# Second MLP layer in five matmuls for six, whole phase tables and wider VectorE operations, in a fused S4D and channel-MLP kernel

## The chip, the cores and the metric

One core of one Trainium2 chip runs the whole program. Its engines are TensorE (PE in the profile), VectorE (DVE), ScalarE (ACT), GpSimd (POOL) and SyncE (SP, which here only issues DMAs); each takes its own instructions in order, and semaphores tie them together. The metric is device microseconds from the start of the program to its end; the median of several runs counts. Float32 results are needed, so the MLP's matmuls run on operands that were split into a rounded high part and a low part (type fp32r).

## The reference

```python
x = A_u                                     # (1, 2048, 576)
xn = layernorm(x)
s = S4D(xn)      # K = 2 Re(sum_n C exp(A dt l)), causal convolution by FFT over 2048 tokens, + xn * D_skip
y = layernorm(xn)
h = gelu(y @ w1 + b1)                       # 576 -> 4608
g = silu(h @ w2 + b2)                       # 4608 -> 576
return x + s * g
```

The MLP reads layer-normed tokens, S4D convolves each of the 576 channels with its own kernel, and the two meet only in the last line.

## The kernel before

**Slots.** The MLP is cut into 48 slots. A slot takes a group of 512 tokens (TB) and 384 hidden units (G = 3 tiles of 128). Its first layer (`layer1`, L599) is three runs of 14 matmuls of 512 columns, each followed by gelu (L635) and by the split into `hh` (ACT, L638) and `hl` (DVE, L641). Its second layer (`layer2`, L662) makes four token tiles j of 128 tokens; for each of the three hidden tiles and each half of the 576 output columns it issues `hh*w2h`, `hh*w2l` and `hl*w2h`, three matmuls of 288 columns: 72 in a slot. Results go to PSUM tiles `mxa` and `mxb` (two banks each, taken in turn), and DVE adds each finished one to `acc` (L672, 576 columns). A bank can be written again only when that add has read it.

**S4D work.** Between the MLP's matmuls stand the parts of S4D: for each block of 16 channels a table (`tables`: phases, sine and cosine on ACT, products on DVE, in tiles `w`, `v`, `U`, `mg`), from which PE makes the convolution kernel (`kgen`, L978); for each of six chunks of 96 channels the transform of x (`x1`, L1082), of the kernel (`k1`, L1113), a second stage and product (`s2`, L1143; `copy`, `prod`, `sums`), the inverse (L1185) and the last transform (`i1`, L1211). `i1`'s two halves are copied out by ACT (L1219) and stored to `s_s` in DRAM by POOL's queue (L1220).

**The end.** For tokens 0 to 7 of each group of 16 (tiles b 0 to 7) the gate is finished half-way through the kernel and `combine` (loads L701 to L703, two DVE operations L709 and L710, stores L713) makes their output. Tiles 8 to 15 wait for the last two slots: `last_s` loads one tile of s from DRAM (SP's queue, L724, 288 KB, each into its place in `A`), and `finish` makes the gate from `acc` (ACT L745, DVE L750 to L756), multiplies, adds x (L760) and issues two stores of 64 rows (L763). The last tile, 15, is done in two halves of 288 columns, straight from PSUM.

**Order.** The program traces itself through a planner (`Order`): each piece is a `step` with an engine, a cost in us, needs and marks; `advance` takes steps in the order of the time that the plan gives them, urgent ones (due times `by`) ahead. The order of each engine's instructions, and of each DMA queue's issues, is fixed by that plan when the program is built. `pe_turns` decides where PE takes a piece of S4D: `pace` and `END` spread the chunks, `DUE` and `ALONE` say when a `kgen` may stand by itself; where it can, it rides ahead of another piece (`ride`). `LEN` holds the planned length of the parts of a slot's second layer, `add_by` when an add must be done. `pair` (L582) does two half-height matmuls of a coming slot at once.

**Memory.** `tile_pool` names share memory: equal names take turns in `bufs` buffers. A table needs its `w` from one of two buffers, and the single `v` and `U`, which are free only when the `kgen` of the block before has run. `row` has four buffers, for `combine` and `finish` alike.

Of the kernel before, what the change touches and what calls it, by code (L numbers as in the profile page):

```python
# [18 lines left out]
P = 128  # L19
# [16 lines left out]
TB = 512  # L36

def dve(n):  # L40
    return 0.075 + 0.00104 * n
# [169 lines left out]
def mixer_kernel(ctx, tc, u, log_a_real, a_imag, c_real, c_imag, log_dt, d_skip, w1, b1, w2, b2,  # L211
# [38 lines left out]
    idp = sb.tile([P, P], F32, name="idp")  # L250
# [112 lines left out]

    def table_memory():

        t = [sb.tile([P, 2, SB, NV], F32, name="w", bufs=2) for _ in range(2)]
        t = [x.rearrange("p k c t -> p (k c t)") for x in t + [sb.tile([P, 2, SB, 64], F32, name="v")]]
        return [t[k // 3][:, k % 3 * D:(k % 3 + 1) * D] for k in range(8)]
# [163 lines left out]
    def split_raw(low_on=nc.vector):  # L532
# [4 lines left out]
        if which == 1:  # L537
            if i == 0 and k:
                w1_tiles()
            h, lo, r1, r2 = W[1]  # L540
            h, lo = (h[:, i], lo[:, i]) if i < KB else (r1, r2)
        else:
            if i == 0:
                W[2] = (sb.tile([P, G, D], F32R, name="w2h"), sb.tile([P, G, D], F32R, name="w2l"))
            h, lo = W[2]
            h, lo = h[:, i], lo[:, i]
# [97 lines left out]
    def layer2(g, tb, j, terms, last, alone=False):  # L644
# [3 lines left out]
        h, lo = W[2]  # L648
# [7 lines left out]
        if alone:  # L656
            z = q[:, terms[0][1], :288]
            nc.tensor.matmul(z, IDM[0], acc[:, tb * 4 + j, terms[0][1] * 288:][:, :288], start=True, stop=False)
        for i, dh in terms:
            d = slice(dh * 288, dh * 288 + 288)  # L660
            for k, (a, b) in enumerate(((hh, h), (hh, lo), (hl, h))):
                nc.tensor.matmul(q[:, dh, :288], a[:, i, c], b[:, i, d], start=i == 0 and k == 0 and not alone,  # L662
                                 stop=i == G - 1 and k == 2)
        if last:
            Q2.pop(j)
        if alone:
            return z

        def add(dh, n):
            o = acc[:, tb * 4 + j].rearrange("p (h d) -> p h d", h=2)[:, dh:dh + n]  # L670
            b = BIAS[0].rearrange("p (h d) -> p h d", h=2)[:, dh:dh + n] if g == 0 else o
            nc.vector.tensor_add(o, q[:, dh:dh + n, :288], b)  # L672
# [97 lines left out]
    def params():  # L770
# [8 lines left out]
        dt = sb.tile([P, 2, SB, 32], F32, name="U").rearrange("p a b c -> p (a b c)")[:, :D]  # L779
# [108 lines left out]
    def tables(b):  # L888
# [5 lines left out]
        def phase(k):  # L894
            if k == 0:
                T["w"] = sb.tile([P, 2, SB, NV], F32, name="w", bufs=2)
# [28 lines left out]
        def weigh(k, part):  # L925

            if k == 0 and part == 0:
                T["v"] = sb.tile([P, 2, SB, 64], F32, name="v")
                T["U"] = sb.tile([P, 2, SB, 32], F32, name="U")
                TAB[b] = (T["U"], T["v"])  # L930
            w, v, m = T["w"], T["v"], T["m"]
            if part == 0:
                nc.vector.tensor_mul(T["U"][:, k], w[:, k, :, 33:], m[:, :, 64:])
            elif part == 1:
                nc.vector.tensor_mul(v[:, k, :, :32], w[:, k, :, 32:0:-1], m[:, :, :32])
            elif k == 0:
                nc.vector.tensor_mul(v[:, k, :, 32:], w[:, k, :, :32], m[:, :, 32:64])
            else:
                nc.vector.scalar_tensor_tensor(v[:, k, :, 32:], w[:, k, :, :32], -1.0, m[:, :, 32:64],
# [6 lines left out]
                 step("DVE", dve(SB * NV), f(phase, 0), need=[("wu", b - 2, 1)] if b > 1 else []),  # L946
# [6 lines left out]
                + [step("DVE", dve(n), f(weigh, k, part), need=[("sin", b, k)] + ([("kg", b - 1)] if b else []),  # L953
                        mark=("wu", b, k) if part == 2 else None) for k in range(2) for part in range(3)])
# [10 lines left out]
    def kgen(b):  # L965
# [20 lines left out]
        return [step("PE", KG + 0.2, mm, need=need + [("wu", b, 1)], cv=1, mark=("kg", b)),  # L986
# [23 lines left out]
    def chunk(c):  # L1010
# [41 lines left out]
        def in_parts(which, i, get, m, need):  # L1052

            def high():
# [655 lines left out]
```

## Time and profile before

| | us |
|---|---|
| median of 3 runs (1099.77 to 1100.17) | 1099.98 |
| span of the profiled execution | 1099.5 |
| PE busy / DVE busy / ACT busy / POOL busy in it | 1090.1 / 920.5 / 696.6 / 184.6 |
| start of the last slot's second layer on PE, in it | 1082.63 |
| start of the last `i1` on PE, in it | 1024.69 |

The profile covers one execution, first to last instruction; its own time is that span, half a microsecond under the median of the timed runs. Matmuls are pipelined and the end of each is modelled, so the pace of PE is read from the distance of starts, and not from the duration of one. DVE's records also overlap: a following operation starts some 0.08 us before the record of the one before ends. The chain of waits follows the work that ended last back through what released it.

### The profile page before, as it was taken

Reading aid. Unit: us, or ns where it says so; the run is one execution under the profiler, and the core shown is the slowest. Engines: PE = TensorE matmul, PEld = TensorE weight load, DVE = VectorE, ACT = ScalarE, POOL = GpSimd, SP = SyncE. Lnnn points to the kernel's source line nnn. Section 1 sums busy time; section 2 is a strip of 40 time slices with the busy share of each in tenths; the row PEclk is TensorE's granted clock in tenths of the full one; section 3 lists DMA queues with packets and bytes.
Section 4 is the critical chain, followed back from the end, with each engine's and each line's share of the span. In section 5 each row is a group of like instructions: output and inputs, shape, how many; then the busy total and the mean of one; then the engine's idle time right before and its main releaser. Section 6 shows DMA issues by size and latency. Waiting matters only on the chain.

```text
span 1099.5 us, 27206 instructions
## 1 busy us (share of the span) xinstructions
PE 1090.1 (99%) x11447; PEld 953.9 (87%) x11447; DVE 920.5 (84%) x1514; ACT 696.6 (63%) x1040; POOL 184.6 (17%) x254
## 2 busy tenths in 40 slices
PE   9999999999999999999999999999999999999997
PEld 7989899889888888888998888888888888888896
DVE  7798678979998899999999998898998986765356
ACT  6585699866666675676865857566675754325233
POOL 5566211170110100001100000000100012110220
PEclk9999999999999999999999999999999999999999
DMA  8746655734444152455623314242333426453453
GB/s 230 235 144 156 232 162 196 215 75 126 154 124 145 48 112 57 116 121 143 150 57 94 91 56 126 39 147 60 90 92 77 143 65 180 117 177 108 126 149 94
DMA packets 139683, 138.23 MB, mean 126 GB/s; under 512 B 88952, under 2 KB 105016, under 8 KB 138984
## 3 DMA queue, kind: packets, MB, share of 16 engines
q1 hardware_dynamic: 124664, 85.49, 29.5%
q0 software_dynamic: 14336, 50.12, 14.8%
q8 instruction: 89, 1.46, 0.6%
q10 hardware_dynamic: 560, 0.89, 0.3%
q14 instruction: 34, 0.28, 0.1%
HBM read 102.17 MB, written 36.63 MB: 126 GB/s over the span
## 4 chain that ended last, share of the span: by engine, by line
PE 96%; SPq 1%; DMA 1%; DVE 1%; issue 0%; ACT 0%; ACTq 0%; DVEq 0%
PE mxb L662 21%; PE mxa L662 21%; PE mxa L599 20%; PE mxb L599 20%; PE cv L1143 3%; PE cv L978 3%; PE cv L1185 2%; PE cv L1211 2%; PE cv L1113 1%; PE cv L1082 1%; DMA w<-in_A_u_dram 1%; SPq L791 1%; PE mxa L614 0%; SPq L383 0%; DMA acc<-in_A_u_dram 0%
## 5 line engine op out<-in xcount | busy, mean ns | idle before, releaser
L641 DVE TENSOR_TENSOR hl<-h,hh 128x512 fp32r<-128x512 f32 x144 | 99.1, 691 | 88.3 <-ACT hh L638 87.6
L662 PE MATMUL mxb<-w2h,hh 128*128 128x288 f32 x576 | 171.6, 298 | 0.0
L662 PE MATMUL mxa<-w2h,hh 128*128 128x288 f32 x573 | 170.8, 298 | 0.0
L662 PE MATMUL mxb<-w2h,hl 128*128 128x288 f32 x576 | 170.1, 295 | 0.3 <-DVE hl L641 0.3
L662 PE MATMUL mxb<-w2l,hh 128*128 128x288 f32 x576 | 169.5, 294 | 0.0
L662 PE MATMUL mxa<-w2h,hl 128*128 128x288 f32 x573 | 169.1, 295 | 0.0
L662 PE MATMUL mxa<-w2l,hh 128*128 128x288 f32 x573 | 168.6, 294 | 0.0
L635 ACT ACTIVATE h<-mxa,b1t 128x512 f32<-128x512 f32 x73 | 50.2, 688 | 111.8 <-PE mxa L599 110.1
L662 PEld LDWEIGHTS mxa<-w2h,hh 128*128 128x128 f32 x573 | 107.6, 188 | 6.6 <-issue 3.5
L662 PEld LDWEIGHTS mxb<-w2h,hh 128*128 128x128 f32 x576 | 108.1, 188 | 5.7 <-issue 1.5
L662 PEld LDWEIGHTS mxb<-w2l,hh 128*128 128x128 f32 x576 | 108.1, 188 | 0.6
L662 PEld LDWEIGHTS mxb<-w2h,hl 128*128 128x128 f32 x576 | 108.1, 188 | 0.5 <-DVE hl L641 0.5
L662 PEld LDWEIGHTS mxa<-w2l,hh 128*128 128x128 f32 x573 | 107.6, 188 | 0.6
L662 PEld LDWEIGHTS mxa<-w2h,hl 128*128 128x128 f32 x573 | 107.5, 188 | 0.0
L879 POOL DMA_DIRECT2D par<-par_s x36 | 27.8, 773 | 464.2 <-DVE mg L922 459.5
L638 ACT ACTIVATE hh<-h 128x512 fp32r<-128x512 f32 x144 | 90.6, 630 | 3.6
L635 ACT ACTIVATE h<-mxb,b1t 128x512 f32<-128x512 f32 x71 | 48.9, 689 | 68.9 <-PE mxb L599 66.5
L672 DVE TENSOR_TENSOR acc<-mxa,acc 128x576 f32<-128x576 f32 x87 | 65.5, 752 | 31.4 <-PE mxa L662 31.0
L672 DVE TENSOR_TENSOR acc<-mxb,acc 128x576 f32<-128x576 f32 x88 | 66.1, 752 | 16.0 <-PE mxb L662 15.5
L599 PE MATMUL mxa<-XH,w1h 128*128 128x512 f32 x284 | 79.1, 400 | 0.0
L599 PE MATMUL mxb<-XH,w1h 128*128 128x512 f32 x280 | 77.8, 399 | 0.0
L599 PE MATMUL mxa<-XL,w1h 128*128 128x512 f32 x284 | 76.1, 390 | 0.0
(261 smaller groups left out, 2485.9 us busy)
## 6 DMA issues: line engine op xcount, KB each, us to landing
raw<-in_B_w_dram SPq DMA_DIRECT2D x72, 288.0 KB, 3.5
raw<-in_B_w_dram SPq DMA_DIRECT2D x96, 192.0 KB, 3.8
par_s<-A POOLq DMA_DIRECT2D x4, 2160.0 KB, 8.2
par<-par_s POOLq DMA_DIRECT2D x36, 240.0 KB, 3.6
f2t<-f2q SPq DMA_DIRECT2D x24, 256.0 KB, 3.3
g2t<-g2p SPq DMA_DIRECT2D x24, 256.0 KB, 4.0
bias<-XR SPq DMA_DIRECT2D x42, 128.0 KB, 3.8
raw<-in_B_w_dram SPq DMA_DIRECT2D x48, 96.0 KB, 4.0
```

The costliest lines, as they stand in the source:

```text
L599: nc.tensor.matmul(q, a, b, start=j == 0 and i not in BEGUN, stop=j == len(ops) - 1, skip_group_check=True)
L635: nc.scalar.activation(t, q, AF.Gelu_apprx_tanh, bias=b1t[:, k:k + 1], scale=1.0)
L638: LAST[0] = nc.scalar.activation(hh[:, i], t, AF.Copy)
L641: nc.vector.tensor_sub(hl[:, i], t, hh[:, i].bitcast(F32))
L662: nc.tensor.matmul(q[:, dh, :288], a[:, i, c], b[:, i, d], start=i == 0 and k == 0 and not alone, stop=i == G - 1 and k == 2)
L672: nc.vector.tensor_add(o, q[:, dh:dh + n, :288], b)
L791: nc.sync.dma_start(r[32 * g:32 * g + 32].rearrange("c (b n) -> c b n", n=32), dram(src[k], 32 * g, [[N, 32], [32 * N, D // 32], [1, 32]]))
L879: nc.gpsimd.dma_start(PAR[b].rearrange("p (g i) k -> p g (i k)", g=4), dram(par_s, (b // 3 * 48 + b % 3 * 4) * NPAR, [[D * NPAR, P], [12 * ...
L978: nc.tensor.matmul(q[32 * g:32 * g + 32, i // 2, i % 2 * 64:i % 2 * 64 + 64], U[:, ri, 4 * g + i, :], v[:, ri, 4 * g + i, :], start=ri == ...
L1143: nc.tensor.matmul(Q[i][32 * q:32 * q + 32, f, 2 * ri:2 * ri + 2], m[r, 4 * i + q, 32 * ri:32 * ri + 32], A2[r, 4 * p + 2 * i + q // 2, :, ...
L1185: nc.tensor.matmul(QI[q // 2][64 * f:64 * f + 64, q % 2, i], MAT["g2t", p + i // 2][r, i % 2, f, ri], YS[p + i // 2][0][r, i % 2, ri, f], ...
L1211: nc.tensor.matmul(Q[h][64 * y:64 * y + 64, t], g1t.rearrange("p a e -> p (a e)"), A2[:, k:k + 2, 1].rearrange("p i d r -> p i r d"), star ...
```

## The change

**Second layer.** The weights of a hidden tile lie side by side, high then low, in one tile `w2` of 3 x 2 x 576 columns. For one hidden tile and token tile, columns 0 to 319 (DA = 320) take three matmuls of 320 columns into the last 320 columns of the first bank, as before in kind. Columns 320 to 575 take `hh` times high and low together (256 + 256 = 512 columns, the whole second bank) and `hl` times high (256 columns): five matmuls for six, over the same 1728 columns. The bank's last 256 columns hold the product with the low part, which a second DVE add (256 columns) puts on `acc`. Token tile 15 of the last slot stays with six.

```diff
-            for k, (a, b) in enumerate(((hh, h), (hh, lo), (hl, h))):
-                nc.tensor.matmul(q[:, dh, :288], a[:, i, c], b[:, i, d], start=i == 0 and k == 0 and not alone,
-                                 stop=i == G - 1 and k == 2)
+            if dh == 0:
+                ops = [(q[:, 0, TB - DA:], a, w[:, i, e, :DA]) for a, e in ((hh, 0), (hh, 1), (hl, 0))]
+            else:
+                ops = [(q[:, 1], hh, w[:, i, :, DA:]), (q[:, 1, :DB], hl, w[:, i, 0, DA:])]
+            for k, (o, a, b) in enumerate(ops):
+                nc.tensor.matmul(o, a[:, i, c], b, start=i == 0 and k == 0, stop=i == G - 1 and k == len(ops) - 1)
...
-        def add(dh, n):
...
-            nc.vector.tensor_add(o, q[:, dh:dh + n, :288], b)
+        def add():
+            o = acc[:, tb * 4 + j]
+            b = BIAS[0] if g == 0 else o
+            nc.vector.tensor_add(o, q.rearrange("p h d -> p (h d)")[:, TB - DA:TB - DA + D], b)
+            nc.vector.tensor_add(o[:, DA:], o[:, DA:], q[:, 1, DB:])
```

**Tables.** A table lies whole in one of two tiles `w` of 2 x 16 x 97 columns; `v` and `U` are gone, and the products are written in place, four operations for six, two of them over 1024 columns. They no longer need the `kgen` of the block before, but the sine and cosine both; the phase of block b needs the `kgen` of block b - 2.

```diff
+    def table_tile():
+        return sb.tile([P, 2, SB, 32 + NV], F32, name="w", bufs=2)
...
+            if part == 0:
+                TAB[b] = (T["w"][:, :, :, 33:], T["v"][:, :, :, :64])
...
+                nc.vector.tensor_mul(v[:, :, :, :32], w[:, :, :, 32:0:-1], bc(m[:, :, :32], 1, 2))
             elif part == 1:
+                nc.vector.tensor_mul(w[:, :, :, 33:], w[:, :, :, 33:], bc(m[:, :, 64:], 1, 2))
+            elif part == 2:
+                nc.vector.tensor_mul(w[:, 0, :, :32], w[:, 0, :, :32], m[:, :, 32:64])
```

**Wider and moved operations.** Transposes after `x1` and `k1` take 768 columns at once (two for four). `prod` and `sums` are one operation each for two, over 768 and 384 columns; for that `copy` also writes a negated part (a second ACT operation of 192 columns). For `x1` POOL first copies x into channel order (`xt`, 768 columns), so that ACT and DVE read straight rows.

```diff
+            def turn():
+                T["x"] = sb.tile([P, 24, m], F32, name="xt")
+                nc.gpsimd.tensor_copy(T["x"], get())
+            def source():
+                return get() if which == "k" else T["x"].rearrange("p c b -> p (c b)")
...
-                for t in range(2):
-                    nc.vector.tensor_mul(PR[i][:, t], bc(Q[i][:, t, 0::2], 2, 2), bc(KK[i][:, t], 1, 2))
+                nc.vector.tensor_mul(PR[i], bc(x, 2, 2), k)
...
-                nc.vector.tensor_sub(y[:, i, 0], x[:, :, 0, 0], x[:, :, 1, 1])
-                nc.vector.tensor_add(y[:, i, 1], x[:, :, 0, 1], x[:, :, 1, 0])
+                nc.vector.tensor_add(y[:, i].rearrange("p a t d -> p t a d"), x[:, :, :, :CH], x[:, :, :, CH:])
```

**Planner.**

```diff
-    LEN = [L1] * G + [3 * n * 0.132 + 0.02 for n in (4, 2, 2, 4, 3, 3, 3, 3)]
+    LEN = [L1] * G + [a * 0.436 + b * 0.343 + 0.02 for a, b in ((2, 2), (2, 0), (1, 1), (1, 3), (3, 0), (0, 3), (3, 0), (0, 3))]
+    ADD = dve(D) + dve(D - DA)
...
-    ALONE, DUE = 12.0, (160.0, 950.0)
+    ALONE, DUE = 12.0, (120.0, 880.0)
```

**The order that the plan makes of it** (read from the two built programs). PE leaves the MLP for a piece of S4D 87 times before and 81 after; `pair` stands 14 times before, 8 after. The first `kgen` stands in slot 7 before, in slot 9 after (slots counted from 0). The end, in the order of each queue:

```
PE before: ... i1, 54 matmuls L2, then three whole slots (42 L1 + 72 L2), the last with tile 15 apart
PE after:  ... 16 L2, i1, 44 L2, then one whole slot (42 L1 + 45 L2, tile 15 apart)
SP before: all eight loads of s (tiles 8 to 15), with weights between, then the stores of tiles 8, 8, 9, 9, ...
SP after:  load 8, load 9, stores of 8 (two), load 10, stores of 9, load 11, stores of 10, load 12,
           stores of 11, load 13, stores of 12, load 14, stores of 13, load 15, stores of 14 and 15
DVE after: adds of slot 46; finish 8; hl 0; combine A; first two operations of 9; hl 1; last of 9; hl 2;
           first two of 10; adds j 0; last of 10; adds j 1; first two of 11; adds j 2; last of 11;
           combine B; finish 12, 13, 14; 15 first half; first operation of its second; combine C; its last
```

Combine A, B and C are the three sets that read the last chunk of S4D for tiles 0 to 7. Before, the loads of s and combine A stand ahead of the last two slots. After, the gate of tile 10 (ACT, L745 before) takes the `row` buffer that the stores of combine A give back, and the loads of B's and C's rows stand on POOL's queue behind the stores of the set before.

More of the change, by code (lines that the diff above doesn't have):

```diff
@@ L36 @@
 TB = 512
+DA = 320
 def dve(n):
@@ L644, in layer2 @@
     def layer2(g, tb, j, terms, last, alone=False):
-        h, lo = W[2]
+        w = W[2]
         hh, hl = HID[tb]
@@ L1636, in mixer_kernel @@
                     add = cell[0]
-                    chain = [step("DVE", dve(D), lambda: add(0, 2), mark=("acc", slot, j), by=add_by(pos, j))]
+                    chain = [step("DVE", ADD, add, mark=("acc", slot, j), by=add_by(pos, j))]
                     if final:
```

103 lines of the change are left out of this document (48 added, 55 removed).

## The prediction

> **What bounds the kernel now.** First the page: how busy each engine is and which of them the chain that ended last consists of.
>
> ```profile
> span 1099.5 us, 27206 instructions
> PE 1090.1 (99%) x11447; PEld 953.9 (87%) x11447; DVE 920.5 (84%) x1514; ACT 696.6 (63%) x1040; POOL 184.6 (17%) x254
> ...
> PE 96%; SPq 1%; DMA 1%; DVE 1%; issue 0%; ACT 0%; ACTq 0%; DVEq 0%
> ```
>
> PE has 96% of the chain, so what PE issues sets the time until its last matmul, and other engines count only where they make it wait or come after it. Then the busy time by stage (PE, PEld, DVE, ACT, POOL), to see how near DVE is to being the bound:
>
> ```profile
> 450.00:750.00 300.00, 299.41 (x3732) 259.84 (x3731) 275.02 (x447) 201.61 (x281) 17.77 (x25) 1.00 0.39 99
> ...
> 900.00:1030.00 130.00, 130.00 (x1371) 110.85 (x1370) 83.60 (x147) 50.55 (x81) 20.11 (x35) 1.00 0.47 133
> 1030.00:1099.00 69.00, 63.14 (x384) 57.74 (x382) 39.25 (x59) 22.61 (x36) 14.90 (x25) 0.99 0.52 140
> ```
>
> In the middle DVE is free for 25 of 300 us, about 2 us in a slot of 24. From 900 on it is free for a third. Last the chain in order of time at the end, which gives PE's pace and the tail:
>
> ```profile
> 1076.29 3.17 PE mxb L599 x14
> 1079.46 3.17 PE mxa L599 x14
> 1082.63 1.58 PE mxb L662 x12
> ...
> 1087.40 2.38 PE mxb L662 x18
> ...
> 1095.08 0.46 DVE v L760
> ```
>
> The last slot's second layer starts at 1082.63; I call this point Z. The span ends at Z + 16.9 (1099.5 - 1082.63): 10.5 of matmuls, then a few DVE operations and stores.
>
> **Part 1: five matmuls for six.** 3.17 / 14 = 0.2264 us for 512 columns, 2.38 / 18 = 0.1322 for 288. The difference over 224 columns is 0.4205 ns a column, and what is left of 0.1322 after 288 columns is 11.1 ns for a matmul as such. The columns stay 1728, so a group loses 11.1 ns: (12 groups x 48 slots - 3 of tile 15) = 573 groups, 6.4 us. A new group is 3 x 0.1457 + 0.2264 + 0.1187 = 0.782 us. No row has 256 or 320 columns under a full weight load. Bounds: the rounding of the two rows allows 11.8 ns, 6.8 us gained; if 256 columns took the 0.1322 of 288, a group would grow by 2.4 ns, 1.4 us lost. I take 6.4, as both rows fit one line and 256 lies near 288.
>
> The Trainium skill ("TensorE: Matmul & The Clock Gate", Back-to-back issue gap) gives an isolated warm matmul N / 2.4 + 2.5 ns. By that the removed matmul would be worth 2.5 ns a group, 1.4 us in all, and the forecast 5 us later. The rows above, 11.1 ns, are of this kernel with its weight loads, and the sum goes by them.
>
> **Part 2: PE's other pieces.** What it costs to leave the MLP for S4D and come back:
>
> ```profile
> 308.17 0.39 PE L599 MATMUL mxb<-XR,w1s 128*128 128x512 f32 x1
> 308.49 1.10 PE L978 MATMUL cv<-v,U 128*32 128x64 f32 x64
> ...
> 311.07 0.40 PE L662 MATMUL mxa<-w2h,hh 128*128 128x288 f32 x1
> 311.30 0.29 PE L662 MATMUL mxa<-w2l,hh 128*128 128x288 f32 x1
> ```
>
> 308.49 - 308.17 is 0.09 over a 512-column pace, 311.30 - 311.07 is 0.10 over a 288-column one: 0.19 for a visit. 87 visits become 81: 1.1 us gained. Six lost pairs cost between nothing and one 512-column matmul each, 0 to 1.4 us; I take 0.6. PE as a whole: -6.4 - 1.1 + 0.6 = -6.9 us.
>
> **Part 3: DVE and POOL in the middle.**
>
> ```profile
> L672 DVE TENSOR_TENSOR acc<-mxb,acc 128x576 f32<-128x576 f32 x88 | 66.1, 752 | 16.0 <-PE mxb L662 15.5
> L1048 DVE TENSOR_TENSOR f2t<-f1t,f2t 128x256 fp32r<-128x256 f32 x6 | 2.5, 418 | 2.9 <-ACT f2t L1045 2.9
> L1158 DVE TENSOR_TENSOR pr<-cv,kk 128x384 f32<-128x384 f32 x96 | 48.7, 550 | 2.0 <-ACT kk L1152 1.8
> L1062 DVE TENSOR_TENSOR ys<-xc,pr 128x768 fp32r<-128x768 f32 x12 | 24.7, 2057 | 2.0 <-ACT pr L1058 2.0
> L1062 DVE TENSOR_TENSOR ys<-kt,pr 128x768 fp32r<-128x768 f32 x12 | 11.1, 928 | 0.0
> ```
>
> Records overlap by 0.08. The second add comes 191 times: 191 x (0.418 - 0.08) = 64.6 us more. Of two operations made one, 2 x 0.550 - 0.928 - 0.08 = 0.09 is saved; 216 such (48 transposes, 48 prod, 48 sums, 72 table products) give 19.9. Straight rows of x save 12 x (2.057 - 0.928) = 13.5. Net 31 us more, 0.65 a slot. The cover is the 2 us a slot that DVE is free; without it PE would wait for `hl` or a bank. The tight place is token tile j 2, which needs the bank of j 0. Between them stands the last work of j 1, 12 x 0.1322 = 1.59 before and 0.438 + 3 x 0.345 = 1.47 after, while the add grows from 0.67 to 1.01: slack 0.92 becomes 0.46. An operation of 1.2 us begun just before then holds PE for up to 0.7. I take +1 us for the whole kernel, between 0 (due times hold) and 6 (a quarter of a us in every second slot).
>
> POOL's copy of x is new. Nearest rows: its 576-column operation, and the DVE operation that ran beside such ones (duration min/median/max in ns).
>
> ```profile
> L432 POOL TENSOR_SCALAR v<-v,mv,rs x2: 2292/2293/2294, 86.5 to 89.8; 128x576 f32<-128x576 f32 x2
> L641 DVE TENSOR_TENSOR hl<-h,hh x144: 626/692/939, 21.8 to 1084.1; 128x512 fp32r<-128x512 f32 x144
> ```
>
> So a copy takes some 3.05 us (2.29 x 768 / 576), and DVE loses at most 0.25 on an operation beside it, some 1 us in each of 12 slots, inside the free 2. ACT (63% busy) has room for 48 short copies. Cost 0; without the cover at most 12 x 1.
>
> The Trainium skill ("SBUF — State Buffer", Who interferes with whom) has a DVE operation with two SBUF inputs and a POOL operation that reads SBUF block each other whole. The row's worst is 0.25, against it; rival (d) is what it would do.
>
> The tables' products no longer wait for the `kgen` before:
>
> ```profile
> L933 DVE TENSOR_TENSOR U<-w,mg 128x512 f32<-128x512 f32 x72 | 49.3, 684 | 3.7 <-PE cv L978 2.3 <-ACT w L914 0.7
> ```
>
> That wait was 2.3 us of DVE in all and none of PE: worth 0.
>
> **Part 4: the end.** Here the order changes most, and this decides.
>
> ```profile
> 1024.69 2.94 PE L1211 MATMUL cv<-A,g1t 128*64 128x384 f32 x16
> ...
> 1033.42 1.28 SPq L724 DMA_DIRECT2D A<-s_s  x3
> ...
> 1040.73 3.19 POOL L713 DMA_DIRECT2D out_dram<-row  x6 [6.98 <-DVE row L710]
> ...
> DMA to landing us min/median/max: 5.2/6.3/6.6
> ...
> w<-u_s SPq DMA_DIRECT2D x6, 288.0 KB, 4.6
> ...
> raw<-in_B_w_dram SPq DMA_DIRECT2D x72, 288.0 KB, 3.5
> ...
> out_dram<-row POOLq DMA_DIRECT2D x16, 48.0 KB, 1.9
> ...
> 1094.39 1.68 ACTq L763 DMA_DIRECT2D out_dram<-v  x2
> ...
> SPq L763 <- DVE w L760: 30.2, 5, 17.9
> ```
>
> The last row is SP's queue: it stands at a store until DVE has made its tile, 30.2 us in five waits, and nothing behind goes out. Before, no load stands behind a store. After, load k + 2 stands behind the stores of tile k.
>
> `i1` starts 2.9 + 44 / 5 x 0.782 + 3 x 3.17 = 19.3 us before Z, for 58 before the change. Load 8 goes out 8.7 after `i1` starts (1033.42 - 1024.69), at Z - 10.6, and lands after 5.2 to 6.6 (the row of the loads of s); with 5.8, at Z - 4.8. All of DVE's queue waits there. Up to the end of tile 11 it then has 12 operations of 0.73 for tiles 8 to 11, three `hl` of 0.6, two of combine A and three adds of 1.05: 15.2 us. It also waits for tile 10's gate, which waits for the stores of A: A is done at Z - 0.5, six issues take 3.2, the last lands 1.4 later, the gate takes 0.7, Z + 4.8, and DVE is there at Z + 3.6: 1.2. Tile 11 ends at Z + 11.6.
>
> From there loads and stores alternate: two store issues 1.1 (0.55 each), load 13, two operations 1.5, two issues 1.1, load 15. A lone load of 288 KB: between 3.5 (weights) and 6.3 (s, four at a time); I take 4.6, the same shape from `u_s`. Load 15 lands at Z + 24.5. Three half operations 1.4, combine C 1.0, four POOL issues 2.1; the end comes 3.4 after the last issue in the trace (1099.5 - 1096.1), here 2.9, as POOL's stores land 0.5 earlier. End at Z + 31.9: 15.0 later than before. With 3.5 and 5.2 for the loads 12.2, with 6.3 and 6.6 19.2. PE itself waits about 2 us in this slot: tile 9's gate on ACT waits for tile 8's second operation, the gelu of hidden tile 1 stands behind it and `hl` 1 comes 1 us late; then the bank of j 0. That is hidden behind the loads.
>
> **Sum.** 1099.5 - 6.9 + 1 + 15.0 = 1108.6 against the span; the median stands 0.5 above its span, so 1109.1.
>
> **Rivals.**
> (a) Not slower: the loads of s are not late. If loads 8 to 15 were in before DVE reaches them, DVE after the add of j 2 (Z + 9) would have 0.7 + 1.5 + 4.4 + 2.4 left and the stores 5: Z + 23, +6.1, 1100.2; where tiles 8 to 11 are done before Z too, 3 less, 1097. It decides if load 15 lands before Z + 16. For it: SP has nothing else to do then. Against: the queue row above. 10%, half of it for each time.
> (b) DVE becomes the bound in the middle: 0.65 us a slot on 2 us free, with the bank of j 0 tighter. At 0.25 us in each of the 36 slots with S4D 9 us for the 1 taken: 1117. For it the 275 of 300; against, the due times and the third that is free from 900 on. 11%.
> (c) The change doesn't do what it says: 256 columns cost as much as 288, PE's 6.4 becomes a loss of 1.4: 1117. For it, no row of that width; against, both widths on one line. 6%.
> (d) POOL's copy stops DVE whole: 12 x (3.05 - 2) = 12 us: 1121. This is the rule of the SBUF page named above. 2%.
>
> **Chances.** The forecast has 71%, its own range 1104 to 1114. From (a) to (d) the range goes to 1101 and 1117. Faster by over 0.2% (2.2 us, about what can be told from no change) 5%, within it 5%, slower 90%.
>
> **What would show it.** Group rows: 320, 512 and 256 columns starting 0.146, 0.226 and 0.119 apart; 256-column adds of 0.42; PE's last matmul near Z + 12, and Z near 1076. Load 15 issued some 20 after Z behind the stores of 13, DVE idle from releases by loads of s, a chain that ends over SP and DMA. Wrong if Z comes at 1083 or later (parts 1 or 3), or the span ends less than 25 after it (part 4).

## The result, and the profile after

The changed kernel takes 1150.5 us (1149.8 to 1152.9) beside 1100.1 for the kernel before on the same chip: ratio 1.0461, 95% interval 1.0446 to 1.0476, 50.5 us slower. The forecast was 1109.1 with a range of 1101 to 1117: the direction held, the size was off by 41 us.

The first lines of the page of the changed kernel:

```profile
span 1148.9 us, 26233 instructions
...
PE 1103.0 (96%) x10874; PEld 927.7 (81%) x10874; DVE 982.9 (86%) x1489; ACT 704.0 (61%) x1095; POOL 214.7 (19%) x266
...
PE 66%; DVE 19%; DMA 6%; issue 4%; ACT 2%; POOL 1%; SPq 1%; DVEq 0%; POOLq 0%; ACTq 0%
```

PE's share of the chain that ended last fell from 96% to 66%, and DVE has 19% of it. DVE works 62 us more than before (982.9 for 920.5), where 31 were forecast. Busy time by stage (PE, PEld, DVE, ACT, POOL, then the granted clock):

```profile
150.00:300.00 150.00, 142.96 (x1039) 122.95 (x1038) 120.53 (x190) 110.14 (x185) 38.02 (x60) 0.98 0.46 138
...
450.00:750.00 300.00, 293.54 (x3211) 243.86 (x3210) 279.13 (x403) 193.45 (x286) 30.24 (x28) 1.00 0.37 97
```

In the middle PE lost 6.5 of 300 us, for 0.6 before, and 7.0 in the stage from 150 to 300 us. What it waited for (us in total, times, longest):

```profile
PE mxb L601 <- DVE acc L681: 6.6, 2, 5.6
PE mxb L673 <- DVE acc L681: 4.0, 6, 1.3
PE mxa L673 <- DVE hl L643: 2.4, 3, 1.4
PE mxb L673 <- DVE hl L643: 2.0, 3, 1.6
```

L681 is the second add, L643 is `hl`. Before, such waits were all but absent; the only one of layer 2 was:

```profile
PE mxb L662 <- DVE hl L641: 0.3, 1, 0.3
```

These are only the waits that outlast a matmul's own time in the records (about 0.3 us). Taken from start to start, layer 2 as a whole grew from 466.2 to 482.8 us of PE and layer 1 from 451.7 to 466.3; of the latter 2.7 are twelve matmuls more, as six fewer pairs are done ahead.

Now the pace of layer 2, from the chain in order of time, where nothing waits:

```profile
305.96 2.38 PE mxa L673 x15
...
329.53 2.38 PE mxb L673 x15
```

Fifteen matmuls take the 2.38 us that eighteen took before: the sixth matmul was worth next to nothing. From start to start, means of the undisturbed ones over the trace: 146.5 ns for 320 columns and 118.0 for 256, as the line through the old rows said, but 234.3 for 512 columns, where layer 1's take 227.9. A group takes 3 x 146.5 + 234.3 + 118.0 = 791.8 ns, for 6 x 132.35 = 794.1 before: 2.3 ns x 573 = 1.3 us in the whole kernel, not 6.4.

Last the end. The rows of the chain from the last inverse transform on, and a row of the timeline that shows where layer 2 of the last slot starts:

```profile
1094.87 2.91 PE cv L1226 x16
...
1098.91 4.48 DMA s_s<-ys
...
1103.52 3.93 DMA A<-s_s
...
1132.01 5.19 DMA A<-s_s
...
1139.97 1.60 POOL out_dram L722 x3
```

```profile
1114.47 0.45 PE L673 MATMUL mxb<-w,hh 128*128 128x320 f32 x2
```

So Z is 1114.5, not 1076. The end is as forecast against Z: `i1` starts 19.7 before it (at 1094.8 on PE; forecast 19.3), the first loads of s go out 11.0 before it (10.6), the last load lands 22.7 after it (24.5), and the span ends at Z + 34.4 (31.9). (An expectation below has 34.7: it counts from the weight load ahead of that matmul.) PE's last matmul started 6.7 us before the end of the span in the kernel before, and 23.3 here.

Of the 49.4 us between the two spans, 32.7 come before PE's last matmul (1092.8 to 1125.6) and 16.6 after it. The end was forecast at 15.0; the forecast for the rest was minus 6. The failure lies in the body.

### The profile page after: what moved, and what is told of

It is laid out like the page before. It is cut to its first block, busy times and chain, and to the rows that moved or that the text cites. A ratio compares the mean times of both kernels' runs of the same rounds, so it can differ in the third digit from the quotient of the medians.

```text
span 1148.9 us, 26233 instructions
## 1 busy us (share of the span) xinstructions
PE 1103.0 (96%) x10874; PEld 927.7 (81%) x10874; DVE 982.9 (86%) x1489; ACT 704.0 (61%) x1095; POOL 214.7 (19%) x266
## 4 chain that ended last, share of the span: by engine, by line
PE 66%; DVE 19%; DMA 6%; issue 4%; ACT 2%; POOL 1%; SPq 1%; DVEq 0%; POOLq 0%; ACTq 0%
PE mxb L673 14%; PE mxa L673 14%; PE mxb L601 14%; PE mxa L601 13%; PE cv L1157 3%; DVE acc L680 3%; PE cv L986 2%; DVE w L943 1%; DVE hl L643 1%; PE cv L1200 1%; DMA kk<-turns_s 1%; PE cv L1099 1%; DVE w1l L551 1%; DVE mg L932 1%; PE cv L1129 1%
## 5 line engine op out<-in xcount | busy, mean ns | idle before, releaser
L673 PE MATMUL mxb<-w,hh 128*128 128x320 f32 (+1 forms) x864 | 237.5, 342 | 4.4 <-DVE acc L681 4.0
L673 PE MATMUL mxa<-w,hh 128*128 128x320 f32 (+1 forms) x855 | 235.0, 342 | 0.1
L673 PE MATMUL mxb<-w,hl 128*128 128x320 f32 (+1 forms) x576 | 170.3, 296 | 2.0 <-DVE hl L643 2.0
L673 PE MATMUL mxa<-w,hl 128*128 128x320 f32 (+1 forms) x570 | 168.8, 296 | 2.7 <-DVE hl L643 2.4
L673 PEld LDWEIGHTS mxb<-w,hh 128*128 128x128 f32 x864 | 148.0, 188 | 26.6 <-issue 7.6
L673 PEld LDWEIGHTS mxa<-w,hh 128*128 128x128 f32 x855 | 146.4, 188 | 21.2 <-issue 5.4
L643 DVE TENSOR_TENSOR hl<-h,hh 128x512 fp32r<-128x512 f32 x144 | 100.0, 695 | 66.7 <-ACT hh L640 66.5
L673 PEld LDWEIGHTS mxb<-w,hl 128*128 128x128 f32 x576 | 108.4, 188 | 2.9 <-DVE hl L643 2.8
L673 PEld LDWEIGHTS mxa<-w,hl 128*128 128x128 f32 x570 | 107.3, 188 | 4.1 <-DVE hl L643 4.0
L601 PE MATMUL mxb<-XL,w1h 128*128 128x512 f32 x280 | 76.0, 394 | 0.0
L601 PE MATMUL mxa<-XH,w1l 128*128 128x512 f32 x284 | 76.0, 389 | 0.0
```

Of the source, the lines that this page charges most:

```text
L601: nc.tensor.matmul(q, a, b, start=j == 0 and i not in BEGUN, stop=j == len(ops) - 1, skip_group_check=True)
L643: nc.vector.tensor_sub(hl[:, i], t, hh[:, i].bitcast(F32))
L673: nc.tensor.matmul(o, a[:, i, c], b, start=i == 0 and k == 0, stop=i == G - 1 and k == len(ops) - 1)
```

## The experiments

Names are those of the labels. Differences are against the kernel before, timed on the same chip.

| kernel | us | over before | ratio, 95% interval | last `i1` starts | PE's last matmul | from there to the end |
|---|---|---|---|---|---|---|
| before | 1100.1 | | | 1024.7 | 1092.8 | 6.7 |
| after | 1150.5 | 50.5 | 1.0461, 1.0446 to 1.0476 | 1094.8 | 1125.6 | 23.3 |
| five_old_order | 1132.1 | 32.2 | 1.0289, 1.0272 to 1.0307 | 1053.8 | 1122.6 | 7.2 |
| old_order_no_low | 1099.1 | -0.8 | 0.9992, 0.9983 to 1.0002 | 1022.7 | 1090.7 | 6.7 |
| old_order_sbuf | 1123.3 | 23.4 | 1.0213, 1.0198 to 1.0228 | 1046.1 | 1114.4 | 7.4 |
| short_first | 1098.6 | -1.8 | 0.9983, 0.9974 to 0.9993 | 1022.2 | 1090.2 | 6.7 |
| straight512 | 1152.7 | 52.8 | 1.0480, 1.0464 to 1.0495 | 1095.3 | 1127.0 | 23.0 |
| no_low_add | 1132.2 | 32.3 | 1.0300, 1.0283 to 1.0316 | 1080.3 | 1111.5 | 22.4 |
| tables_wide | 1101.6 | 1.2 | 1.0012, 1.0002 to 1.0021 | 1022.6 | 1093.1 | 6.3 |
| tables_wide_copy | 1107.5 | 7.1 | 1.0063, 1.0048 to 1.0078 | 1022.3 | 1099.2 | 6.4 |
| six_kept | 1107.4 | 7.5 | 1.0070, 1.0055 to 1.0085 | 1022.5 | 1099.4 | 6.3 |
| copy_on_act | 1101.2 | 1.1 | 1.0011, 1.0001 to 1.0020 | 1032.4 | 1093.0 | 6.4 |
| five_act_order | 1131.2 | 30.9 | 1.0280, 1.0262 to 1.0297 | 1061.4 | 1122.7 | 6.9 |
| six_plan | 1144.6 | 44.2 | 1.0401, 1.0385 to 1.0416 | 1057.6 | 1135.3 | 6.8 |
| plan_no_add | 1155.6 | 55.2 | 1.0510, 1.0490 to 1.0530 | 1087.1 | 1145.6 | 7.1 |
| loads_together | 1151.9 | 52.0 | 1.0474, 1.0458 to 1.0490 | 1093.7 | 1124.4 | 24.2 |
| turns_14 | 1167.2 | 67.3 | 1.0611, 1.0594 to 1.0629 | 1114.8 | 1125.7 | 41.8 |
| no_copy | 1174.7 | 74.5 | 1.0670, 1.0652 to 1.0688 | 1120.3 | 1123.8 | 49.5 |
| no_copy_no_low | 1161.5 | 61.3 | 1.0548, 1.0531 to 1.0566 | 1106.3 | 1109.8 | 50.2 |
| due_before | 1152.7 | 52.5 | 1.0476, 1.0461 to 1.0492 | 1095.1 | 1127.1 | 23.2 |

The last three columns are from each kernel's profiled execution; the kernels without the second add, and old_order_sbuf, leave the low product of columns 320 to 575 out of the sum.

### One half of the change at a time

**five_old_order.** The kernel before with the five matmuls and the second add; every queue keeps its order.

```diff
-        def add(dh, n):
+        def add():
...
+            nc.vector.tensor_add(o[:, DA:], o[:, DA:], q[:, 1, DB:])
...
-    chain = [step("DVE", dve(D), lambda: add(0, 2), ...
+    chain = [step("DVE", dve(D), lambda: add(), ...
```

> The kernel before with only the five matmuls and the second add; tables, transposes, x and the planner's costs and due times as before, so that every engine keeps the order of before. Two theories for the 31.6 us that layer 2 of the last slot starts later after the whole change. Theory A (the second add: 0.34 us of DVE, 191 times, on an engine that was 92% busy in the middle, makes PE wait for hl and for banks): this kernel is slower than before by 15 to 35 us, and PE's waits for DVE acc and hl appear here. Theory B (the new order: setup work packed otherwise, products of tables and S4D earlier or later): the order is the old one, so PE waits as little as before; 1.3 us less from the pace seen after (791.8 ns a group for 794.1) and at most 5 more for the adds, 1099 to 1104. Both: 512-column matmuls of layer 2 start 234 apart as after.

**six_kept.** The changed kernel with the old `layer2`, `LEN` and add.

> The changed kernel with the six matmuls of 288 columns and the one add of 576 put back (and the planner's costs of these); whole tables, wide operations, the copy of x on POOL and the earlier due times stay. Theory A (the second add): the stalls in the body go, the late end stays: 1100 + about 15, 1112 to 1120. Theory B (the new order): nearly all stays, 1140 to 1150, with the 6 us wait of PE near 161 us still there.

Theory A holds: the first is 32.2 us over before, the second only 7.5. The waits of PE in five_old_order:

```profile
PE mxb L671 <- DVE acc L679: 4.1, 5, 1.9
PE mxa L671 <- DVE acc L679: 2.5, 5, 1.1
PE mxa L671 <- DVE hl L641: 2.1, 4, 0.8
PE mxa L582 <- DVE acc L679: 1.4, 3, 0.7
```

The order is that of before and the waits are those of after; what is new in them is the second add (L679 here) and the `hl` behind it. The long stall near 161 us is not in five_old_order, and the last slot's layer 2 starts 57 us after `i1`, so the end is as short as before. In six_kept the stall is gone too and the end is 6.3, against both theories, which had left the one or the other there: both come only where the planner counts five matmuls and two adds.

### The price of the second add

**no_low_add, old_order_no_low.** The line of the second add left out, in the changed kernel and in five_old_order.

```diff
-            nc.vector.tensor_add(o[:, DA:], o[:, DA:], q[:, 1, DB:])
```

> The changed kernel without the second add (the low product of columns 320 to 575 is left out of the sum); order and planner's costs as in the changed kernel. Theory A (the adds make PE wait): 191 x 0.34 = 65 us of DVE gone, 10 to 25 us faster than the changed kernel, 1125 to 1140. Theory B (the order): the waits of PE for hl, w and XL and the one of 6 us stay, at most 8 us faster, 1142 or more.

> As five_old_order (the order of before, five matmuls), but without the second add: the low product of columns 320 to 575 is left out of the sum. Theory A1 (all of the 32 us of five_old_order is the second add on DVE): back to 1098 to 1101, PE's last matmul near 1092. Rival A2 (the five matmuls themselves, with 512 columns that hold a bank to their end and hl needed earlier in a group, cost PE waits too): 1105 to 1115.

**old_order_sbuf.** In five_old_order the second add reads SBUF.

```diff
-            nc.vector.tensor_add(o[:, DA:], o[:, DA:], q[:, 1, DB:])
+            nc.vector.tensor_add(o[:, DA:], o[:, DA:], o[:, :DB])
```

> As five_old_order, but the second add reads 256 columns of acc in SBUF in place of the low product in PSUM (the low product is left out, another number is added): DVE has as many operations of about that length, but the bank is free after the first add. Theory A-throughput (DVE, 92% busy in the middle, gets 5 to 6% more work and falls behind): 1120 to 1132, as five_old_order. Rival A-latency (the bank that is freed 0.34 later is what PE waits for): 1100 to 1110.

Without the add, five_old_order falls back to 1099.1: A1, the whole price is the add's. It is 1132.1 - 1099.1 = 33.0 us, for the 74.7 us that DVE is busier (994.8 for 920.1). The rest of five_old_order, the matmuls, is worth 0.8, in line with the 1.3 of the pace. With the bank free after the first add 24.2 of the 33.0 stay and 8.8 go: the time is in the range of the throughput theory, but the bank has a share. What PE waits for moves, as the waits of old_order_sbuf show:

```profile
PE mxa L671 <- DVE hl L641: 3.6, 6, 1.3
...
PE mxb L599 <- ACT h L635: 1.3, 1, 1.3
...
PE mxa L671 <- DVE acc L678: 1.0, 2, 0.8
```

It is now `hl`, and ACT's gelu, that are late.

Where PE loses the time can be read from the distance of its starts, against old_order_no_low. Of 31 us in five_old_order 15 are lost at the first two matmuls of token tile j 2, the place that the prediction took for the tight one, and 5.5 at the first matmul of the layer 1 that follows; the rest is spread over `hh`, `hl` and other banks. With the bank free early, j 2 costs 4 of 22 us. The place is tight even where DVE takes both adds at once, as in this slot of five_old_order (the end of j 0, the end of j 1, the start of j 2, and the adds of j 0):

```profile
209.32 0.28 PE L671 MATMUL mxb<-w,hl 128*128 128x256 f32 x1
...
210.82 0.28 PE L671 MATMUL mxa<-w,hl 128*128 128x256 f32 x1
211.00 0.54 PE L671 MATMUL mxb<-w,hh 128*128 128x320 f32 x2
```

```profile
209.64 0.76 DVE L678 TENSOR_TENSOR acc<-mxb,acc 128x576 f32<-128x576 f32 x1
210.43 0.42 DVE L679 TENSOR_TENSOR acc<-acc,mxb 128x256 f32<-128x256 f32 x1
```

The second add ends at 210.85, and j 2 starts at 211.00, 0.18 behind the matmul ahead of it for the usual 0.12; the next start is 0.07 late as well. In all 45 slots of five_old_order where j 2 follows j 1 without a piece of S4D between, its start is at least 0.057 us late; in old_order_no_low in none. The second add reads what the first wrote, and starts 0.03 after that record ends, not 0.08 before: the pair keeps DVE for 1.12 us (0.78 and 0.34), where the one add before kept it for 0.67.

In the changed kernel the same line is worth 18.3 us (1150.5 - 1132.2), within theory A's range but less than in the order of before; the late end stays (22.4).

**five_act_order.** copy_on_act (below) with the five matmuls and the second add, in the order of copy_on_act.

> copy_on_act with the five matmuls and the second add, in the order of copy_on_act: no copy on POOL, DVE 28 us less busy than in the kernel before. Theory K1 (the second add costs what does not fit on DVE): of its 33 us only 5 to 20 are left, 1105 to 1121. Rival K2 (its price is that of single late adds, whatever DVE's mean load is): 1125 to 1135.

K2 holds: 29.8 us over copy_on_act (1101.2 on its chip, with 1100.2 for before there, 1100.4 here). The stage from 450 to 750 us:

```profile
450.00:750.00 300.00, 293.62 (x3177) 243.01 (x3176) 274.86 (x408) 207.82 (x297) 16.94 (x24) 1.00 0.37 96
```

DVE works 274.9 of 300 us there, as in the kernel before (275.0), and PE loses 6.4, for 0.6 before. So the free share of DVE is no cover. Here too 15 us are lost at j 2's first two matmuls. DVE's queue is in order, its operations are released one by one by PE and ACT, and what stands behind an add has a time by which PE needs it. In all the orders tried the second add stands right behind the first; whether it would be free at a later place of the slot was not tried.

### The 512-column matmul

**straight512.** In the changed kernel the moving operand is one stretch.

```diff
-                ops = [(q[:, 1], hh, w[:, i, :, DA:]), ...
+                ops = [(q[:, 1], hh, w[:, i].rearrange("p e d -> p (e d)")[:, DA:DA + TB]), ...
```

> The changed kernel, but the 512-column matmul reads 512 neighbouring columns (high 320 to 575 and then low 0 to 255) in place of two stretches of 256 that lie 576 apart; so the low product of columns 320 to 575 is one with other weights. Order and sizes are the same. Theory C (the two stretches cost PE the 6.5 ns by which 234.3 lies over layer 1's 227.8): 512-column matmuls of layer 2 start 227.8 apart, 573 x 6.5 = 3.7 us less of PE, the time 2 to 4 us below that of the changed kernel. Rival (what a mix of widths costs, or the weight load beside it): 234 stays, and the time with it.

**short_first.** In old_order_no_low the order of the two is turned around for the middle hidden tile.

```diff
+            if dh and 0 < i < G - 1:
+                ops = ops[::-1]
```

> As old_order_no_low (order of before, no second add, its low product left out), with the 256-column matmul ahead of the 512-column one in the middle of the three hidden tiles. Theory P1 (a 512-column matmul takes 6.5 ns longer to the next start because a 256-column one that adds to the same bank follows it): in those groups the 512-column one starts 228 ahead of the next and the sum of the pair falls to about 346. Rival P2 (any pair of these two widths costs 352): the sum stays. The time stays within 0.2% of old_order_no_low either way (191 x 6.5 ns = 1.2 us at most).

Theory C falls: 234.4 from start to start with one stretch. P1 falls and P2 holds: in the turned groups the 512-column matmul starts 235 ahead of the next, not 228, and over all groups the pair takes 352.3 as before (233.8 and 118.5). So 6.5 ns lie on layer 2's 512-column matmul, whatever follows it and however its columns lie; why, stays open.

### Tables, wide operations and the copy of x

**tables_wide_copy, tables_wide, copy_on_act.** Six matmuls and the old due times; x copied by POOL, not copied, or copied by ACT.

```diff
-                nc.gpsimd.tensor_copy(T["x"], get())
+                nc.scalar.activation(T["x"], get(), AF.Copy)
...
-                four.append(step("POOL", 2.3, turn, need=need))
+                four.append(step("ACT", act(2000), turn, need=need))
```

> The kernel before with the whole tables, the wide operations and POOL's copy of x, but with its six matmuls and its due times: six_kept with the due times of before. Theory D1 (six_kept's 7.4 us are the price of the earlier due times): 1096 to 1101. Rival D2 (they are the price of the wider operations, 0.95 and 1.2 us long, behind which hl or a bank waits): 1104 to 1109.

> As tables_wide_copy, but x is split from where it lies, without POOL's copy (2.05 us of DVE for 0.97, 12 times, 13 us more of DVE and 37 us less of POOL). If POOL's copy slows DVE down or is late for the split of x, this one is faster by 1 to 4 us; if DVE's time counts, slower by 1 to 6 us.

> tables_wide_copy (six matmuls, whole tables, wide operations) with x turned by ACT in place of POOL, 12 times some 2.1 us on an engine that is 63% busy, nothing left out. Theory F1 (POOL's copy holds DVE up): no DVE operation is held, DVE has 13 us less than in tables_wide, 1097 to 1101, so below the kernel before or level with it. Rival H2 (ACT is late for h and hl in turn): 1102 to 1108.

D1 falls: the due times are worth nothing with six matmuls (1107.5 with the old, 1107.4 with the new). D2 has the time, but not the cause: whole tables and wide operations cost 1.2 us (0.2 to 2.3 by the interval), POOL's copy 5.9 more (7.1 - 1.2), and the same copy on ACT nothing. copy_on_act lies between F1 and H2 (1101.2): nothing is held, and nothing is gained. The reason stands in the timelines of POOL and DVE in tables_wide_copy (start, length, operation):

```profile
382.86 2.49 POOL L1059 COPY xt<-xc 128x768 f32<-128x768 f32 x1 [11.35 <-DVE ys L1071]
```

```profile
382.71 0.69 DVE L643 TENSOR_TENSOR hl<-h,hh 128x512 fp32r<-128x512 f32 x1
383.60 3.10 DVE L643 TENSOR_TENSOR hl<-h,hh 128x512 fp32r<-128x512 f32 x2 [0.20 <-ACT hh L640]
```

The first `hl` begins ahead of the copy and takes its usual 0.69, and the copy takes 2.49 for its usual 2.10; the next `hl`, issued inside the copy, takes 2.29 (two together 3.10) and ends 0.55 after the copy does. In this kernel 11 DVE operations with two operands in SBUF were held in this way beside its 12 copies, 20 us together over their usual length. An operation that reads PSUM beside a copy keeps its length (the 576-column add from 804.95: 0.75). This is the rule of the Trainium skill ("SBUF — State Buffer", Who interferes with whom) that the prediction set aside for the trace's 0.25; the trace here agrees with it for a copy, and not for the norm's operation (last section).

In the changed kernel POOL's and DVE's rows and PE's next wait near 581 us are:

```profile
581.07 2.10 POOL L1066 COPY xt<-xc 128x768 f32<-128x768 f32 x1
```

```profile
579.68 4.05 DVE L932 TENSOR_TENSOR mg<-par 128x1024 f32<-128x1024 f32 x2
583.65 0.68 DVE L643 TENSOR_TENSOR hl<-h,hh 128x512 fp32r<-128x512 f32 x1
```

```profile
584.39 0.42 PE L673 MATMUL mxb<-w,hl 128*128 128x320 f32 x1 [1.55 <-DVE hl L643]
```

Two `mg`, as a rule 1.22 (1024 columns) and 0.68 (512), take 4.05, `hl` behind them is late, and PE stands 1.55 us. The stalls that end at 269, 416, 719 and 855 us come 4 to 8 us after the start of a copy too; they were not followed step by step.

copy_on_act and tables_wide also show that DVE's time is worth nothing where PE does not wait for it: DVE is 28 and 17 us less busy than in the kernel before (892.0 and 903.8 for 920.5), and the kernel is not faster. No complete version was below the kernel before: the best are these two at 1.0011 and 1.0012.

**no_copy, no_copy_no_low.** The changed kernel without POOL's copy, and without the second add as well.

> The changed kernel without POOL's copy of x: x is split from where it lies, as before (2.05 us of DVE for 0.97, 12 times). In the trace of the changed kernel eight DVE operations that read two operands in SBUF stood still until a copy beside them was over, 15.1 us in all, and the stalls of PE at 269, 416, 584, 719 and 855 us come right behind. Theory F1 (the blocked operation is late for hl or a bank, and PE waits): those stalls go, and the time falls by 6 to 14 us, to 1137 to 1145, though DVE's own work grows by 13. Rival F2 (DVE's work counts, whoever holds it): 15.1 saved for 13 added, within 3 us of the changed kernel.

> As no_copy, and without the second add (its low product left out). If the second add and the copy explain the whole of the 50 us, this is within 5 us of the kernel before but for the late end (PE's last matmul at 1093 to 1098, then 15 to 22 us): 1108 to 1118. If the order itself makes PE wait, PE's last matmul is at 1105 or later.

F1 and F2 both fall: 24 us slower than the changed kernel. PE's last matmul comes a little earlier, 1123.8. But look at the last inverse transform in no_copy, the chain in order of time:

```profile
1120.33 1.55 PE cv L1217 x8
...
1122.77 1.62 PE cv L1217 x8
...
1156.82 5.40 DMA A<-s_s
...
1164.62 1.60 POOL out_dram L722 x3
```

It is PE's very last work, and loads of s, gates and stores of all eight last tiles come after it. The planner counts 2000 columns for each split of x here, on ACT and on DVE, and puts S4D's pieces later; that it lacks room on DVE is likely, but was not shown. no_copy_no_low is out of its range too (1161.5), with PE's last matmul at 1109.8: by its own mark the order itself makes PE wait. Neither run says what the copy costs in the changed kernel; they say that the order answers an edit more strongly than the edit itself.

### The order and the end

**due_before, loads_together, turns_14, plan_no_add**, all from the changed kernel:

```diff
-    ALONE, DUE = 12.0, (120.0, 880.0)
+    ALONE, DUE = 12.0, (160.0, 950.0)
```

```diff
-        c3["steps"].append(step(None, 5.0, lambda k=k: last_s(k), need=[("st", NCH - 1), ("x8", k)], mark=("s8", k)))
+        c3["steps"].append(step(None, 0.6, lambda k=k: last_s(k), need=[("st", NCH - 1), ("x8", k)]))
+    for k in range(8):
+        c3["steps"].append(step(None, 0.6 if k else 5.0, lambda: None, mark=("s8", k)))
```

```diff
-    gl["steps"].append(step(None, 5.0, lambda: None, mark="turns"))
+    gl["steps"].append(step(None, 14.0, lambda: None, mark="turns"))
```

```diff
-    ADD = dve(D) + dve(D - DA)
+    ADD = dve(D)
```

> The changed kernel with the due times of before (160 and 950 us). With six matmuls these changed nothing (1107.47 with the old, 1107.38 with the new ones). Theory G1 (they are idle here too): 1148 to 1153. Rival G2 (the earlier due times pull S4D's first half forward and hold DVE up then): the 6 us stall near 161 goes, 5 to 10 us faster.

> The changed kernel with the eight last loads of s issued one behind another on SP's queue, ahead of all stores, for one load, two stores, one load; nothing else moved before the last slot. Theory T1 (the part 4 of the prediction: the end is late because each load stands behind the stores of a tile): the span ends about 20 us after layer 2 of the last slot starts for 34.7, so 10 to 15 us faster than the changed kernel, 1136 to 1141. Rival T2 (DVE's work itself, late with the rest, sets the end; the loads land in the same time anyway): at most 4 us faster.

> The changed kernel with 14 us for 5 planned for the transfer of the small table kk (turns), so that DVE's three odd-row steps are placed later; nothing is left out. Theory S1 (DVE stands 6 us at that transfer near 157 us, the adds behind it hold a bank, and PE stands 6.0 us and then runs at half clock for some 2.3 more): the stall near 161 goes, 6 to 9 us faster, 1141 to 1145. Rival S2 (DVE is behind there anyway, and the stall shows up elsewhere): at most 3 us faster.

> The changed kernel, but the planner counts an add of 576 columns alone; the second add still runs, nothing is left out. The planner then puts the last inverse transform and the loads of s earlier. Theory E1 (the late end, 23.3 us after PE's last matmul for 6.7, comes from the planner's place for the last inverse transform, which the second add's planned time pushes to 19 us before layer 2 of the last slot): the end takes 7 to 9 us after PE's last matmul again; the body waits as in the order of before, PE's last matmul at 1118 to 1128, 1128 to 1138 in all. Rival E2 (DVE's real work pushes the end, whatever the plan says): the end stays above 15 us, 1140 or more.

G1 holds for the due times (nothing gained, 2 us more). loads_together refutes T1. SP sends the eight loads together at 1103, those in the trace have landed by 1112.5, and the time stays. The end of its chain shows what comes next:

```profile
1131.92 6.14 DMA row<-g_s
...
1139.62 1.61 POOL out_dram L722 x3
```

Combine C's loads go out on POOL's queue behind the stores of combine B, land at 1138.1, and the stores follow. T2 has the time, but DVE's work alone does not set it: DVE stands 4.18 us until those loads are in. Two chains of the same length end the kernel, and the prediction had named one of them.

turns_14 aims at the longest stall of PE, whose cause is this row of DVE in the changed kernel:

```profile
157.36 0.23 DVE L295 TENSOR_TENSOR kk<-kk 128x64 f32<-128x64 f32 x1 [5.95 <-DMA kk<-turns_s]
...
160.78 0.42 DVE L681 TENSOR_TENSOR acc<-acc,mxb 128x256 f32<-128x256 f32 x1
```

DVE stands 5.95 us at a small transfer of the setup, the adds of a bank stand behind it, and PE waits 5.63 for that bank. With 14 us planned the stall is gone, as S1 has it; but PE's last matmul does not move (1125.7), and the last `i1` comes after the last slot's layer 1. The end takes 41.9 us, and the kernel loses 17 more. In plan_no_add the last `i1` is 48 us ahead of Z again and the end is 7.1, as E1 said; but the body pays 20 us more, and the whole is 5 us slower.

**six_plan.** The whole change in the order for six matmuls and one add.

> The whole change, but the order that the planner makes for six matmuls and one add (the order of six_kept): its costs for layer 2 and for the add are the old ones. Theory J1 (what the single prices, 33.0 for the second add in the old order and 7.4 for the rest, leave of the 50.6 us is the planner's order with a last inverse transform that comes late): the end takes 7 us after PE's last matmul, and the prices add up or less, since wider operations leave DVE 20 to 33 us of room: 1125 to 1140. Rival J2 (they hinder one another in any order: POOL's copy and the second add on one engine): 1145 or more.

Of J1 the end holds (6.8), but the prices do not add up to the time or less: 44.2 for 39.3. 1144.6 lies between the two ranges, at J2's edge.

## Why the prediction was wrong

The 50.5 us, by the runs: the matmuls -0.8, the second add 33.0, tables and wide operations 1.2, POOL's copy 5.9, together 39.3. In one order that knows nothing of the five matmuls they make 44.2 (six_plan); the 4.9 between are for hindering one another or for that order, which is not quite the one of before, and were not separated. The planner's own order adds 6.3 (50.5 - 44.2): PE's last matmul 9.7 earlier, the end 16.5 longer. The split depends on the order in which it is taken: in the changed kernel's own order the second add is worth 18.3, and without it PE's last matmul is still nearly 19 later than before and the end 15.7 longer.

- **Part 3, the step that failed**: "slack 0.92 becomes 0.46", and with it "I take +1 us for the whole kernel, between 0 (due times hold) and 6". The place was right, the slack was not. The working set the adds alone against j 1's work; it left out that j 0's last matmul still runs for 0.16 us in the record when j 1's work begins (0.28 less the pace of 0.12) and that 0.15 pass from the end of the adds to the matmul that waits for them, and it let the second add overlap the first, which it doesn't (1.12 for 1.01). From the start of j 0's last matmul to j 2's first it takes 1.68 with nothing late, and PE is there after 1.62. So a slot loses some 0.13 there even then, and a late operation on DVE comes on top: 15 us in five_old_order. Wrong too was the cover, "the 2 us a slot that DVE is free": five_act_order shows that a DVE with the mean load of before in the middle does not cover it either. Measured: 33.0 us, of which freeing the bank after the first add takes away 8.8; the other 24.2 come from the time on DVE, with what stands behind it late. Rival (b) had place and kind, but at a quarter of a us in 36 slots it had 9 us.
- **Part 3, DVE's sum**: 31 us more were forecast, 62 came. The second adds are 74.7 for 64.6, the operations that copies held some 15 for 0, and the savings 28 for 33 (copy_on_act).
- **Part 3, POOL's copy**: "Cost 0; without the cover at most 12 x 1". Measured 5.9 with six matmuls. The rows used were of another POOL operation, the norm's, beside which `hl` keeps near its length; a copy holds such an operation until it is over. The mechanism is rival (d)'s, which had 2% and 12 us. That its size is not further off is luck: it took a copy of 3.05 us less 2 us of free DVE, and the copy takes 2.10. That it also costs about that in the changed kernel was not shown, since no_copy changed the order.
- **Part 3, fewer and wider operations**: the 28 us of DVE that they save were worth no time; with six matmuls PE hardly waits for DVE.
- **Part 1**: 6.4 us forecast, 1.3 by the pace and 0.8 by old_order_no_low. 320 and 256 columns lay on the line through 288 and 512; the 512-column matmul of layer 2 did not repeat layer 1's 0.2264 but took 0.2343. The estimate of 1.4 us from the gap of the Trainium skill ("TensorE: Matmul & The Clock Gate", Back-to-back issue gap) is what came out, but by luck: by its formula for an isolated matmul 256 columns would start 109.2 ns apart, and they take 118.0.
- **Part 2** was not tested by itself. 81 visits stood in the trace, as forecast; the six lost pairs cost 0.3 by its starts (2.7 us more in layer 1, 2.4 less in pairs), where 0.6 was taken.
- **Part 4** was right in kind and size (16.6 for 15.0, Z + 34.4 for 31.9). That loads alternate with stores is one of two chains of the same length there, so taking it away gained nothing; what makes the end long is how late the last `i1` is put. Each kernel with `i1` 48 us or more ahead of the last slot's layer 2 ends 6.3 to 7.4 us after the start of PE's last matmul.

By the marks set ahead, Z at 1083 or later says parts 1 or 3 are wrong: it came at 1114.

## What to carry over

An operation added to an in-order queue is not covered by that engine's mean free time: 33 of the 75 us that the second adds took on DVE reached PE while DVE was 92% busy, and with DVE freed of 28 us elsewhere the five matmuls and the add still cost 29.8 for 32.2. Price such an edit by what stands behind it in its queue and by when that is needed; work the slack out from start to start, with the end of the work ahead and the release in it; and try the edit alone in the old order before the planner is told of it. Where a planner writes the order, a change of its costs is an edit of its own, to be measured apart.

## What the runs showed of the hardware

A copy on POOL from SBUF to SBUF holds a DVE operation with two operands in SBUF until it is over, at times even one whose record begins earlier (starts on POOL are rough): a table product of tables_wide_copy ran from 368.87 to 372.07, 3.20 us for 0.68, around a copy from 369.41 to 371.51, and ended 0.56 after it, like those that begin inside. The norm's TENSOR_SCALAR on POOL did not do so: beside the one from 61.36 to 63.95 in the kernel before two `hl` took 0.68 and 0.64, and of the 17 operations with two operands in SBUF that ran beside the norm's there for over 0.3 us none took over 0.34 longer than usual.

The hold works the other way too. One copy of the changed kernel began while such an operation ran, and eight more followed on DVE without a gap, at their usual lengths; the last of the nine ended at 734.08, and the copy took 7.17 us for 2.10:

```profile
728.85 7.17 POOL L1066 COPY xt<-xc 128x768 f32<-128x768 f32 x1 [11.25 <-DVE ys L1078]
```

After PE's wait of 5.63 us in the changed kernel, its matmuls of layer 1 start 0.43 apart for 4.7 us (groups of four; the last row shows the usual pace again):

```profile
161.34 2.05 PE L601 MATMUL mxb<-XH,w1h 128*128 128x512 f32 x4 [5.63 <-DVE acc L681]
163.19 1.91 PE L601 MATMUL mxb<-XL,w1h 128*128 128x512 f32 x4
...
167.14 1.08 PE L601 MATMUL mxa<-XH,w1h 128*128 128x512 f32 x4
```

Eleven of them at 426 to 427 ns are 2.2 us over the usual 228; the granted clock is 0.50 from 160 to 166.7 us and 1.00 before and after. The Trainium skill ("TensorE: Matmul & The Clock Gate", The HAM clock gate) states half rate after an idle window of about 3.4 us; the trace agrees.
